# Four more 128-column dummy matmuls on TensorE ahead of the first projection

## The chip, the cores and the metric

The kernel runs on one core of one Trainium2 chip. The metric is device time in microseconds (us). The profile's granted clock does not show the start: in the view by windows it reads 1.00 from the first us on, while the first 4 us of matmuls come at half the later rate, so "slow" and "full" clock below are read from the spacing of matmuls.

Names of engines in the profile: PE is TensorE (matmuls), PEld its weight loads, DVE VectorE, ACT ScalarE, POOL GpSimd, SP the queue that issues most DMAs. L939 is line 939 of the kernel.

## The reference, cut to what matters

```python
xn = layernorm(x)                                   # x: 2048 x 512, bf16
out = x + ssm(xn) + (gelu(xn @ w_gate) * (xn @ w_up)) @ w_down
# ssm: a diagonal complex scan over 2048 steps, with projections into and out of the state
```

Only the beginning matters here: the first 128-row tiles of `x` are centered, transposed, and multiplied by the gate and up weights, which are 512 x 1376 and arrive by DMA in slices of 128 rows ("k slices").

## The kernel before

TensorE has nothing to compute for the first 4 us. It is kept busy with matmuls of constants: seven warm-up matmuls of 512 columns, then `fill(n)`, which is n matmuls of 128 columns. One dummy stands ahead of the first transpose and four behind it.

```python
nwarm = 7
...
PE(fwarm, d_pe([512] * nwarm) * 1.6, [], [BANK[wb]], "warm")      # L932
def fill(n):
    def f(e):
        ins_ = None
        for _ in range(n):
            ins_ = e.matmul(PS[wb][:, 0:128], ones, ones, start=True, stop=True)   # L939
        return ins_
    PE(f, 56.0 * n, [], [BANK[wb]], "fill")
...
ch(V(... tensor_reduce(SUM0, X[0]) ...))       # DVE: sum of the first x tile, L965
ch(cent(0, 0), cent(0, 1))                     # DVE: centers it, L960
fill(1)
ch(cent_T(0, 0, 1, 7, "V"))                    # PE: transpose "T0", L679; DVE copies it out, L688
ch(cent(1, 0), cent(1, 1))
fill(4)
...
ks(0, 0, [0], True)                            # PE: first projection, k slice 0, L700
cent_T(1, 0, 1, 6)
ks(0, 0, [1])
cent_T(0, 1, 4, 7)
...
for j in range(2):
    ks(1, j, [0, 1])                           # k slice 1
...
cent_T(2, 0, 4, 7)                             # four transposes
for j in range(2):
    ks(2, j, [0, 1])                           # k slice 2: "the third slice"
```

These loads go out on the SP queue, in this order (x tile 1 goes out on ScalarE's); GT_k (L700) waits for the gate and the up weights of its slice:

```python
ld_x0(0)
...
for k in range(KD):                            # KD = 4
    if k in (1, 3):
        ld_x0((k + 3) // 2)                    # x tile 2 ahead of slice 1, x tile 3 ahead of slice 3
    ld_wk(WG, WGc, ins["B_w_gate"], k)         # 128 KB each
    ld_wk(WU, WUc, ins["B_w_up"], k)
```

PE and the SP queue keep program order. The order on the other engines is chosen by the kernel's own scheduler from declared durations (the 56.0 * n above).

## Time and profile before

| | before |
|---|---|
| time, median of 3 runs | 177.44 us (177.3 to 177.45) |
| span of the profiled execution | 175.7 us (its time: 176.98 us) |
| PE busy | 172.1 us, 98% of the span |

From the page of the kernel before: the span, PE's line of part 1 (busy us, share, instructions), and the engines of the chain that ended last in part 4.

```profile
span 175.7 us, 2494 instructions
...
PE 172.1 (98%) x868; PEld 84.0 (48%) x883; DVE 159.8 (91%) x279; ACT 95.5 (54%) x185; POOL 10.7 (6%) x24
...
PE 98%; issue 1%; DVE 0%
```

PE is the chain. A change at the start counts only as far as it moves everything behind it. The timeline of PE in the first 11 us (columns: start, duration in us, engine, line, operation, out<-in, shape, count):

```profile
0.77 3.15 PE L932 MATMUL PS<-const-bfloat16-1.0 128*128 128x512 bf16 x7 [0.77 <-PEq L1089]
3.71 0.31 PE L939 MATMUL PS<-const-bfloat16-1.0 128*128 128x128 bf16 x1
3.87 0.29 PE L679 MATMUL PS<-arena 128*128 128x128 bf16 x1
3.95 0.51 PE L939 MATMUL PS<-const-bfloat16-1.0 128*128 128x128 bf16 x4
4.57 0.38 PE L700 MATMUL PS<-arena 128*128 128x256 bf16 x2
...
6.95 0.39 PE L679 MATMUL PS<-arena 128*128 128x128 bf16 x4
7.42 2.75 PE L700 MATMUL PS<-arena 128*128 128x512 bf16 x12
...
11.10 0.38 PE L711 MATMUL PS<-arena 128*128 128x512 bf16 x1
```

Matmuls overlap: a duration is a latency (219 ns for each of the four transposes at 6.95), and the distance between starts is the rate (56 ns). The four transposes that begin at 6.95 have their last start at 7.12, so the next matmul could start at 7.18. It starts at 7.42. That is the wait for the third slice: by the trace's landing times its up weights land at 7.288 (a load has landed when the last update of its semaphore has come). The dummies by themselves (the view of one line; duration in ns, minimum, median and maximum):

```profile
L939 PE MATMUL PS<-const-bfloat16-1.0 x5: 218/284/314, 3.7 to 4.2; 128*128 128x128 bf16 x5
```

314 ns is a dummy at the slow clock and 218 ns one at the full clock, so in this execution the clock opened within the run of dummies. The single starts put it between 4.16 and 4.24. The slow spacing is 107 ns for 128 columns and the full one 56; the Trainium skill, "TensorE: Matmul & The Clock Gate", section "Back-to-back issue gap", gives N / 1.2 and N / 2.4 + 2.5 ns, which is 107 and 56, and this trace agrees. In the chain of waits the tail then runs without an interruption of more than 0.05 us (the longest pieces: start, us, what):

```profile
7.42 2.75 PE PS L700 x12
10.40 0.86 PE PS L700 x4
11.26 6.93 PE PS L711 x40
18.24 5.13 PE PS L842 x23
```

### The profile page before, as it was taken

The numbers are of one execution on the slowest core, as the hardware profiler recorded it, in microseconds if no ns is written. First come the engines' busy times: TensorE is split into PE (matmuls) and PEld (weight loads), VectorE is DVE, ScalarE is ACT, GpSimd is POOL, SyncE is SP. The second block draws the span as 40 slices with busy tenths as digits, with TensorE's granted clock in tenths as the row PEclk, the third lists the DMA queues.
The fourth block names the chain that finished last, engine by engine and source line by source line (L and its number), as shares of the span: only waits on it lengthen the run. The fifth ranks groups of instructions, "written<-read, shape, count | busy, mean of one in ns | idle before, by whom it ended". The sixth has DMA issues, their size and how long they took to land.

```text
span 175.7 us, 2494 instructions
## 1 busy us (share of the span) xinstructions
PE 172.1 (98%) x868; PEld 84.0 (48%) x883; DVE 159.8 (91%) x279; ACT 95.5 (54%) x185; POOL 10.7 (6%) x24
## 2 busy tenths in 40 slices
PE   8999999999999999999999999999999999999995
PEld 3545564644544444444644444444464444444454
DVE  6987999996999989889899999989999899999941
ACT  5476677899876898383576792000667970000000
POOL 3122030201000000002100000000000000000000
DMA  5899999695998000002015000002001000000311
GB/s 155 241 320 174 215 178 222 126 132 113 191 298 225 0 4 2 0 30 85 8 39 111 1 0 0 4 0 90 30 0 30 4 0 0 0 0 0 120 64 60
DMA packets 32420, 14.36 MB, mean 82 GB/s; under 512 B 23736, under 2 KB 32408, under 8 KB 32408
## 3 DMA queue, kind: packets, MB, share of 16 engines
q1 hardware_dynamic: 32240, 14.07, 35.5%
q8 instruction: 7, 0.11, 0.3%
q10 hardware_dynamic: 168, 0.13, 0.2%
q14 instruction: 5, 0.04, 0.1%
HBM read 6.46 MB, written 2.10 MB: 49 GB/s over the span
## 4 chain that ended last, share of the span: by engine, by line
PE 98%; issue 1%; DVE 0%
PE PS L883 37%; PE PS L842 32%; PE PS L748 16%; PE PS L711 4%; PE PS L700 3%; PE PS L816 3%; PE PS L932 2%; PE PS L679 1%; PE PS L939 0%; DVE arena L901 0%
## 5 line engine op out<-in xcount | busy, mean ns | idle before, releaser
L883 PE MATMUL PS<-arena 128*128 128x512 bf16 (+3 forms) x317 | 65.9, 366 | 0.3
L842 PE MATMUL PS<-arena 128*128 128x512 bf16 x257 | 57.1, 379 | 0.4
L883 PEld LDWEIGHTS PS<-arena 128*128 128x128 bf16 (+1 forms) x323 | 30.8, 98 | 35.2
L842 PEld LDWEIGHTS PS<-arena 128*128 128x128 bf16 x264 | 25.8, 98 | 30.2
L786 DVE TENSOR_TENSOR_SCAN arena<-arena 128x512 bf16<-128x512 f32 x32 | 38.9, 1255 | 0.0
L857 ACT ACTIVATE arena<-PS 128x512 bf16<-128x512 f32 x33 | 19.8, 599 | 25.8 <-DVE arena L901 16.7
L748 PE MATMUL PS<-arena 128*128 128x512 bf16 (+1 forms) x134 | 28.0, 366 | 0.1
L861 ACT ACTIVATE arena<-PS 128x512 bf16<-128x512 f32 x33 | 19.8, 600 | 5.1 <-PE PS L842 5.1
L875 ACT ACTIVATE PS<-arena 128x512 f32<-128x512 bf16 (+2 forms) x17 | 9.6, 581 | 19.7 <-DVE arena L901 19.0
L748 PEld LDWEIGHTS PS<-arena 128*128 128x128 bf16 x136 | 13.3, 98 | 14.1
L757 ACT ACTIVATE arena<-PS 128x512 bf16<-128x512 f32 x32 | 17.7, 592 | 2.1 <-PE PS L748 2.1
L901 DVE TENSOR_TENSOR arena<-PS,arena 128x512 bf16<-128x512 f32 (+2 forms) x17 | 10.9, 653 | 6.4 <-PE PS L883 6.4
L863 DVE TENSOR_TENSOR arena<-arena 128x512 bf16<-128x512 bf16 x33 | 13.1, 416 | 1.7 <-ACT arena L861 1.6
L775 DVE TENSOR_TENSOR arena<-arena 128x4096 bf16<-128x4096 bf16 (+1 forms) x5 | 9.2, 1859 | 0.8 <-ACT arena L606 0.8
L773 DVE TENSOR_TENSOR arena<-arena 128x4096 bf16<-128x4096 bf16 (+1 forms) x5 | 9.2, 1859 | 0.1
L798 DVE TENSOR_TENSOR arena<-arena 128x4096 bf16<-128x4096 bf16 x4 | 9.2, 2288 | 0.1
L799 DVE TENSOR_TENSOR arena<-arena 128x4096 bf16<-128x4096 bf16 x4 | 9.1, 2284 | 0.0
L720 ACT ACTIVATE arena<-PS,arena 128x256 bf16<-128x256 f32 (+1 forms) x16 | 6.6, 448 | 3.9 <-PE PS L700 2.1
L610 DVE BATCH_NORM_STATS2 arena<-arena 128x6 f32<-128x512 bf16 x12 | 7.7, 679 | 0.1
L711 PE MATMUL PS<-arena 128*128 128x512 bf16 (+1 forms) x40 | 7.1, 336 | 0.0
L723 DVE SCALAR_TENSOR_TENSOR arena<-PS,arena 128x256 bf16<-128x256 f32 (+1 forms) x16 | 6.3, 445 | 0.5 <-PE PS L700 0.5
L700 PE MATMUL PS<-arena 128*128 128x512 bf16 (+1 forms) x28 | 6.2, 349 | 0.2
(96 smaller groups left out, 124.6 us busy)
## 6 DMA issues: line engine op xcount, KB each, us to landing
out_dram<-arena SPq DMA_DIRECT2D x15, 128.0 KB, 1.7
arena<-in_A_x_dram SPq DMA_DIRECT2D x3, 512.0 KB, 5.3
arena<-in_B_w_down_dram SPq DMA_DIRECT2D x1, 1280.0 KB, 7.2
arena<-in_B_w_gate_dram SPq DMA_DIRECT2D x4, 128.0 KB, 3.0
arena<-in_B_w_up_dram SPq DMA_DIRECT2D x4, 128.0 KB, 3.1
arena<-in_B_w_gate_dram SPq DMA_DIRECT2D x1, 480.0 KB, 6.5
arena<-in_B_w_up_dram SPq DMA_DIRECT2D x1, 480.0 KB, 7.4
arena<-arena SPq DMA_TRANSPOSE x25, 3.1
```

The costliest lines, as they stand in the source:

```text
L700: PE(lambda e: e.matmul(dst, XCd(j, k), WGU[:, ws[0]:ws[-1] + 1, k, f0:f1], start=first, stop=k == KD - 1, skip_group_check=True), d_pe([w ...
L711: ins_ = e.matmul(dst, XCd(j, k), WGU[:, :, k, f0:f1], start=(k == 0), stop=(k == KD - 1))
L748: ins_ = e.matmul(PS[bank][:, 128 * j0:128 * j1], BBT[c][dk].ap[:, 128 * s:128 * (s + 1)], XNT[b].ap[:, dk, 128 * j0:128 * j1], start=(dk ...
L757: GATE["evBu"] = ACT(lambda e, bank=bank, k3=k3, s=s, c=c: e.activation(SSc[k3][s][c].ap, PS[bank][:, :], ACTF.Copy), d_act(512), [BANK[ba ...
L786: V(lambda e, g=g, rb=rb, init=init: e.tensor_tensor_scan(g.ap, rb, g.ap, init, ALU.mult, ALU.add), d_dve_scan(512), [g, PA[RRr]] + ([CARc ...
L842: ins_ = e.matmul(PS[bank][0:m, c0:c1], W.ap[:, dk, 128 * ft:128 * ft + m], XNT[b].ap[:, dk, c0:c1], start=(dk == 0), stop=(dk == KD - 1))
L857: GATE["last_gelu"] = ACT(lambda e, bg=bg, kk=kk, m=m: e.activation(GG[kk].ap[0:m, :], PS[bg][0:m, :], ACTF.Gelu_apprx_tanh), d_act(512), ...
L861: ACT(lambda e, bu=bu, kk=kk, m=m: e.activation(UPB[kk].ap[0:m, :], PS[bu][0:m, :], ACTF.Copy), d_act(512), [BANK[bu]], [UPB[kk]], "evU")
L863: V(lambda e, kk=kk, m=m, ft=ft, k2=k2: e.tensor_tensor(HTt[k2][ft].ap[0:m, :], GG[kk].ap[0:m, :], UPB[kk].ap[0:m, :], ALU.mult), d_dve_tt ...
L875: ACT(lambda e: e.activation(PS[bank][:, c0:c1], X[tt].ap[:, c0:c1], ACTF.Copy), d_act(c1 - c0), [X[tt]], [BANK[bank]], "seed")
L883: ins_ = e.matmul(PS[bank][:, c0:c1], l_[:, 128 * j:128 * (j + 1)], r_[:, c0:c1], start=False, stop=last and n == len(ops) - 1, skip_group ...
L901: V(lambda e: e.tensor_tensor(OUTB[ko].ap[:, c0:c1], PS[bank][:, c0:c1], XD[tt].ap[:, c0:c1], ALU.add), d_dve_1x(c1 - c0), [BANK[bank], XD ...
```

## The change

Two dummies are added in each of the two gaps. The intent, as I read it, is to leave PE less idle while it waits, in the hope of an earlier or safer full clock.

```diff
         ch(cent(0, 0), cent(0, 1))
-        fill(1)
+        fill(3)
         ch(cent_T(0, 0, 1, 7, "V"))
         ch(cent(1, 0), cent(1, 1))
-        fill(4)
+        fill(6)
```

## The prediction

> What bounds the kernel now. TensorE does: the page gives PE 172.1 us busy of a 175.7 us span (98%), and the chain of waits that ended last is PE for 98% of the span. From 11.10 us on the chain shows PE without any gap over 0.05 us. So a change at the start is worth what it moves that 11.10 us, and nothing else.
>
> What the start looks like (PE in the timeline of the first 11 us). Seven warm-up matmuls run from 0.77 us, 427 ns apart; the first dummy starts at 3.71; the transpose T0 at 3.87, released by the first centering on DVE; four dummies from 3.95 to 4.24 (starts 107, 106 and 74 ns apart); then PE idles until the first projection at 4.57, which waits for DVE's copy of the transpose (4.20 to 4.43). The 74 ns step and the fall of a dummy's duration from 314 to 218 ns put the change to the full clock at 4.17 to 4.24 us, 3.4 us after the first matmul. The Trainium skill, "TensorE: Matmul & The Clock Gate", Part 1, says that about 3.4 us of sustained activity opens the clock gate; this trace agrees. From 4.57 us on everything already runs at full speed (256 columns 108 ns apart). So the dummies have nothing left to win here, in this execution: before 4.17 they can't open the clock sooner, since the warm-up has been dense since 0.77.
>
> What is added. Two dummies ahead of T0, at the slow clock: 107 ns each. They'd run at 3.82 and 3.92, so T0 starts at about 4.03 in place of 3.87: 0.16 us late, as there was only 0.055 us of room. The DVE copy and the first projection slide with it, to about 4.73. Two dummies behind T0: 56 to 107 ns each; they end before 4.60, still ahead of 4.73, so they cost nothing by themselves. PE work, slot time: about 0.33 us in all; nothing is removed, no DMA moves. The order on the other engines should stay as it is.
>
> What of it is on the critical path. The 0.16 us slide runs through the first and second k slices, until PE must wait for the third slice of the up weights. Landing times in the trace: its DMA lands at 7.29 us; PE's last transpose was issued at 7.12 and would have let the next projection start at 7.18, but it starts at 7.42. So PE holds 0.25 us of slack there, more than the slide of 0.16 us, and DMA issues do not depend on PE this early. I expect the projection at 7.42 to stay, and the tail at 11.10 to stay within 0.05 us.
>
> Predicted: 177.45 us, with a range of 177.0 to 178.0 us; faster by over 2% 0.015, within 2% 0.97, slower by over 2% 0.015.
>
> What would show the steps right: in the profile after, nine dummies in place of five; T0 at 4.0 to 4.1; the first projection at 4.65 to 4.8; the clock change still near 4.2; the projection ahead of which PE idled still at 7.4; the forty-matmul group at 11.1; a span of 175.5 to 176.2.
>
> What would make it wrong: the clock change falling later in the timed runs than in this profiled one (176.98 us against 177.44 in the timed ones hints at variation), where denser dummies could open it earlier and win some tenths, up to half of a 3.4 us window; a third-slice landing that is earlier in the timed runs, so that the 0.16 us shows; or the scheduler putting DVE and ScalarE work in another order, which could move either way by some tenths.

## The result, and the profile after

| | before | after |
|---|---|---|
| time, median | 177.41 us (177.3 to 177.45, 6 runs) | 177.36 us (177.15 to 177.66, 6 runs) |
| ratio | | 1.0000, 95% interval 0.9987 to 1.0013 |
| span of the profiled execution | 175.7 us | 176.3 us (its time: 177.62 us) |

A ratio is the mean time of one kernel's runs over that of the other's in the same rounds, so it is not quite the ratio of the medians. Here the means are 177.39 and 177.39 us: the same, with an uncertainty of about 0.23 us (0.13% of 177). The page after:

```profile
span 176.3 us, 2502 instructions
...
PE 172.8 (98%) x872; PEld 84.9 (48%) x887; DVE 159.7 (91%) x279; ACT 95.5 (54%) x185; POOL 10.7 (6%) x24
...
PE 98%; issue 1%; DVE 0%
```

The span is 0.6 us longer, although the times are equal. So the two profiled executions differ by more than the two kernels do, and the first question is by what. PE's timeline after:

```profile
0.77 3.15 PE L932 MATMUL PS<-const-bfloat16-1.0 128*128 128x512 bf16 x7 [0.77 <-PEq L1089]
3.71 0.53 PE L939 MATMUL PS<-const-bfloat16-1.0 128*128 128x128 bf16 x3
4.03 0.31 PE L679 MATMUL PS<-arena 128*128 128x128 bf16 x1
4.14 0.85 PE L939 MATMUL PS<-const-bfloat16-1.0 128*128 128x128 bf16 x6
4.78 0.63 PE L700 MATMUL PS<-arena 128*128 128x256 bf16 x2
...
7.80 0.39 PE L679 MATMUL PS<-arena 128*128 128x128 bf16 x4
8.02 2.75 PE L700 MATMUL PS<-arena 128*128 128x512 bf16 x12
```

The first projection's two matmuls take 0.63 us here and 0.38 before: they run at the slow clock. All nine dummies do too:

```profile
L939 PE MATMUL PS<-const-bfloat16-1.0 x9: 314/314/314, 3.7 to 4.7; 128*128 128x128 bf16 x9
```

The single starts put the opening of the clock between 6.06 and 6.26, 2 us later than before. The third slice starts at 8.02, without a wait: the last transpose of the four starts at 7.97, one spacing of 56 ns earlier. The tail moves by what the third slice moves, and nothing changes behind it (a piece of this view starts where the one before it ends, hence 8.19 here for the start at 8.02):

```profile
8.19 2.59 PE PS L700 x12
11.00 0.86 PE PS L700 x4
11.86 6.93 PE PS L711 x40
18.84 5.13 PE PS L842 x23
```

The up weights of the third slice landed at 7.752 in this execution and at 7.288 before. Had PE been on time, the third slice would have started 0.135 us behind the landing, as it did before (7.423 - 7.288), at 7.887. So of the 0.60 us between the two profiles, 0.46 is a later DMA landing, and 0.13 is PE arriving later than that landing. Neither is obviously the dummies' work. Twelve experiments were made to settle it.

### The profile page after: what moved, and what is told of

Its sections match the earlier page's. It is cut to its first block, busy times and chain, and to the rows that moved or that the text cites. A ratio compares the mean times of both kernels' runs of the same rounds, so it can differ in the third digit from the quotient of the medians.

```text
span 176.3 us, 2502 instructions
## 1 busy us (share of the span) xinstructions
PE 172.8 (98%) x872; PEld 84.9 (48%) x887; DVE 159.7 (91%) x279; ACT 95.5 (54%) x185; POOL 10.7 (6%) x24
## 4 chain that ended last, share of the span: by engine, by line
PE 98%; issue 1%; DVE 0%
PE PS L883 37%; PE PS L842 32%; PE PS L748 16%; PE PS L711 4%; PE PS L700 3%; PE PS L816 3%; PE PS L932 2%; PE PS L679 1%; PE PS L939 1%; DVE arena L901 0%
## 5 line engine op out<-in xcount | busy, mean ns | idle before, releaser
L748 PE MATMUL PS<-arena 128*128 128x512 bf16 (+1 forms) x134 | 28.0, 366 | 0.1
L711 PE MATMUL PS<-arena 128*128 128x512 bf16 (+1 forms) x40 | 7.1, 337 | 0.0
L723 DVE SCALAR_TENSOR_TENSOR arena<-PS,arena 128x256 bf16<-128x256 f32 (+1 forms) x16 | 6.3, 445 | 0.7 <-PE PS L700 0.7
L700 PE MATMUL PS<-arena 128*128 128x512 bf16 (+1 forms) x28 | 6.8, 373 | 0.0
```

What stands on the lines that cost most here:

```text
L700: PE(lambda e: e.matmul(dst, XCd(j, k), WGU[:, ws[0]:ws[-1] + 1, k, f0:f1], start=first, stop=k == KD - 1, skip_group_check=True), d_pe([w ...
L711: ins_ = e.matmul(dst, XCd(j, k), WGU[:, :, k, f0:f1], start=(k == 0), stop=(k == KD - 1))
L748: ins_ = e.matmul(PS[bank][:, 128 * j0:128 * j1], BBT[c][dk].ap[:, 128 * s:128 * (s + 1)], XNT[b].ap[:, dk, 128 * j0:128 * j1], start=(dk ...
```

## The experiments

Three theories at the outset. **A** (the prediction's): the dummies push the first transpose T0 back, and the wait for the third slice takes that up. **B**: the dummies themselves move the moment at which the clock opens. **C**: that moment varies from one execution to the next, whatever the dummies. From the first four runs theory A was put in numbers, as **A2**, which the later expectations quote.

The first four ran on one chip, the next four on another, the last four on a third; each group shares 11 runs of the kernel before (medians 177.45, 177.34 and 177.19 us).

### The kernel before again, and the changed kernel again

No edit in either.

> The kernel before, unchanged, as a control. Theory A (my prediction: dummies don't move the clock; T0's slide of 0.16 us is taken up by the wait for the third weight slice): time ratio 1.000, the clock in the profile opens at 4.2 us as in the first profile of this kernel, PE idles again about 0.2 us ahead of 7.4. Theory C (the moment when the clock opens varies from one execution to the next, whatever the dummies): the clock opens at another moment than 4.2 us in this profile, anywhere between 4.2 and about 7.6, and the span follows it, up to 0.6 us longer.

Measured: 177.47 us median (177.2 to 178.41), ratio 1.0011 (0.9986 to 1.0037) against itself: this is the resolution of five rounds. In this profile the clock opened between 4.28 and 4.34 us, so it does not tell A from C. But the span is 176.2 us, not 175.7. The third slice started at 7.839, exactly 0.135 us behind a landing at 7.704; PE's wait ahead of it had grown from 0.25 to 0.55 us (last transpose at 7.235). So the weights' landing alone moved the unchanged kernel by 0.42 us at this point; 0.16 more came behind it, 0.14 of it as a wait of PE that ended at 32.9 us.

> The changed kernel again. Its first profile opened the clock at 6.1 to 6.2 us, 2 us later than before's 4.2. Theory B (the dummies themselves move the opening): it opens at 6.1 to 6.2 again and the single times stay about 177.4. Theory C (it varies by execution): it opens at some other moment; single times spread over 0.5 us (177.15 to 177.66 as in the first six runs), ratio to before within 0.2%.

Measured: 177.28 us median (177.05 to 177.71), ratio 0.9996 (0.9977 to 1.0015). The clock opened between 3.92 and 4.12, not at 6.1 to 6.2. Theory B, as expected here, fails: with the same nine dummies the clock opened 2 us sooner. The first x tile landed late (3.065 us against 2.816), and T0 at 4.12 was waiting for it and not for the dummies: the timeline shows the three dummies of the first gap done starting by 3.92.

### Each half of the change, and no dummies at all

```diff
-        fill(1)            # first gap only
+        fill(3)
```

> Only the first half of the change: two more dummies ahead of T0. Theory A: T0 at 4.03 in place of 3.87, first projection at 4.7, ratio 1.000 (within 0.1%), tail group at 11.1 if the clock opens by 4.3. If nothing took the slide up, +0.16 us (+0.09%).

Measured: 177.35 us median, ratio 1.0001 (0.998 to 1.0023). T0 at 4.037 and the first projection at 4.756, as expected. The clock opened between 4.25 and 4.35. The last transpose started at 7.313, so PE would have been ready at 7.37; the weights landed at 7.406 and the third slice started at 7.541, again landing + 0.135. A wait of 0.17 us was left. This execution shows the absorption that the prediction described: T0 late, third slice set by the landing. But the dummies made T0 late by only 0.04 us in it (4.037 against 2.940, the landing of the first x tile, plus 1.056, which the DVE work behind it takes). The tail was at 11.21, not at 11.1, because the landing was later.

```diff
-        fill(4)            # second gap only
+        fill(6)
```

> Only the second half of the change: two more dummies behind T0. With the clock open by about 4.3 they end before the first projection can start (DVE's copy sets it): cost 0. With a late clock (it opened at 5.3 to 6.2 us in six of ten profiles) six dummies of 107 ns end 0.03 us or so too late. Ratio 1.000, within 0.1%.

Measured: 177.33 us median, ratio 1.0006 (0.9984 to 1.0029). The clock opened between 5.95 and 6.05. The first projection started 0.72 us behind T0; without any dummies and with a late clock, the next run, it is 0.70. The price of the second half is at most some hundredths. The profiled execution was a long one (178.36 us), in part because its third slice came at 7.97, and in part (0.84 us) for a reason far from the change, which its view of waits for line 748 names:

```profile
  DMA arena<-arena: 0.7, 1
```

A transpose by DMA of the second block of x landed at 33.55 us, and PE stood still until 33.69. It is a second wait for a DMA, 25 us behind the third slice, which appears in some executions (0.14 us in the control above) and not in others.

```diff
-        fill(1)
...
-        fill(4)
```

> No dummies at all in the two gaps: PE then idles from about 3.71+0.43 to the first projection. Theory A and C: T0 still at 3.87, first projection at 4.57, ratio 1.000 within 0.1% on the mean, as PE has slack later anyway. Theory B (denser PE opens the clock sooner): the clock opens up to 3.4 us later on average, ratio 1.002 to 1.006.

Measured: 177.51 us median (177.22 to 178.9), ratio 1.0017 (0.9989 to 1.0045). The clock opened between 5.94 and 6.14. T0 at 4.005 waited for the first x tile, which landed at 2.950. One profile with a late clock does not show that the dummies' absence made it late, as the kernel with nine dummies was as late; the ratio is inside the control's interval. Left undecided by itself.

### Twenty more: how much does a dummy cost?

The declared length of the fill stays that of one dummy, so that the order of everything else stays.

```diff
-        fill(1)
+        fill(21, 1)        # 21 issued, declared as 1
```

> 21 dummies ahead of T0 in place of 1, the same declared length, so the order of everything else stays. Theory A2 (from the first runs: the third weight slice starts at the later of PE's arrival, T0 + 3.30 us, and the landing of its last DMA + 0.135 us; T0 starts at the later of the end of the dummies and the landing of the first x tile + 1.056 us): the dummies end at about 5.14 if the clock opens at 4.2, T0 at 5.14, PE arrives at about 8.4, later than landing + 0.135 (7.34 to 7.89 so far), so the third slice starts without a wait and the time rises by 0.5 to 1.1 us, ratio 1.003 to 1.006. A theory in which dummies are free, as PE is never late: ratio 1.000. If each dummy cost its slot in full: 5 of 107 ns and 15 of 56 ns, 1.4 us, ratio 1.008.

Measured: 178.64 us median (177.95 to 178.86), ratio 1.0064 (1.0044 to 1.0085); by the means, 178.52 against 177.36, 1.16 us longer. PE's timeline:

```profile
3.71 2.20 PE L939 MATMUL PS<-const-bfloat16-1.0 128*128 128x128 bf16 x21
5.75 0.22 PE L679 MATMUL PS<-arena 128*128 128x128 bf16 x1
...
8.77 0.39 PE L679 MATMUL PS<-arena 128*128 128x128 bf16 x4
8.99 2.75 PE L700 MATMUL PS<-arena 128*128 128x512 bf16 x12
```

The mechanism is as expected and the size a little above it. The third slice started at 8.99 without a wait, 1.49 us later than landing + 0.135 (7.368 + 0.135), and behind it nothing differs from before. The size exceeds the expected range because the clock opened late again, between 5.42 and 5.52, so most of the twenty added dummies took 107 ns. T0 is 1.80 us later than where the landing of the x tile (2.898, plus 1.056 of DVE work and hand-over) would have let it start; the time rose by 1.16. So dummies are neither free nor paid in full: the room ahead of the third slice takes a part.

This run says something else as well. PE issued matmuls back to back from 0.77 us on, and the clock still took 4.65 us to open. Denser work did not make it early.

### Taking the wait away

The third and fourth slices multiply by the second slice's weights (a wrong result), and the waits for the later weights are dropped. The order of all engines is the same.

```diff
-  WGU[:, ws[0]:ws[-1] + 1, k, f0:f1], start=first
+  WGU[:, ws[0]:ws[-1] + 1, min(k, 1), f0:f1], start=first
...
+        late = [S.last_w[c[k].name] for c in (WGc, WUc) for k in (2, 3)]
+        for op in S.ops:
+            if op.tag == "GK":
+                op.deps = [d for d in op.deps if d not in late]
```

> The kernel before, in which the third and fourth slices of the first projection multiply by the second slice's weights, so that nothing waits for the later weights; wrong results on purpose. Theory A2: the gap of 0.25 us ahead of the third slice is gone, PE goes through from T0 to T0 + 3.2 to 3.4 us, the tail group begins 0.1 to 0.5 us sooner, ratio 0.997 to 0.9995. If the landing is not what ends that gap: the gap stays, ratio 1.000.

Measured: 177.59 us median, ratio 1.0009 (0.9994 to 1.0024). The expectation of a gain failed; the measured interval leaves at most 0.1 us of it. In its profile the gap is gone, but there was nothing to win: the clock opened between 6.03 and 6.19, PE reached the third slice at 7.775, and the weights, landed at 7.29, would have let it start at 7.425. Two further things stood ready to take a gain back: a new wait of 0.08 us ahead of the tail group, seen in this run and the next and in no other, and the later DMA waits described above.

> The same for the changed kernel; wrong results on purpose. Theory A2: with the wait gone the dummies' slide is no longer taken up: the third slice starts at T0 + 3.2 to 3.4 us with T0 at 4.03 or later, so 0 to 0.16 us later than in the kernel before without the wait, as far as the first x tile lands early; on time the two differ by less than can be told (0.1%). Ratio to before 0.997 to 1.000.

Measured: 177.41 us median (5 runs), ratio 1.0008 (0.9993 to 1.0024). The clock opened between 5.32 and 5.44; the third slice started at 7.672, when landing + 0.135 would have been 7.54. T0 to third slice is 3.64 us, outside the expected 3.2 to 3.4, because part of it ran at the slow clock. In this execution PE then waited 0.34 us near 18.5 us for the last transpose of the first x block (landed 18.55; the view of waits names DVE's L723, whose semaphore was only looked at behind that one). The pair does not measure the dummies' slide. What it shows is that "PE has slack ahead of the third slice" is at most a property of executions with an early clock, and not of the kernel.

### Making the wait certain

First, one load moved ahead of the third slice's weights:

```diff
-            if k in (1, 3):
-                ld_x0((k + 3) // 2)
+            if k in (1, 2):
+                ld_x0(k + 1)
```

> The kernel before with the fourth x tile loaded ahead of the third weight slice and not behind it; the order of all engines is the same. Theory A2: the third slice's last weights land one transfer of 128 KB later, about 0.35 us; the third slice starts at that landing + 0.135 us, and the time rises by 0.2 to 0.4 us (ratio 1.001 to 1.0025), more in executions with an early clock. If PE's own work sets the time: 1.000.

Measured: 177.46 us median, ratio 1.0009 (0.9991 to 1.0027): inconclusive. The landing came at 7.545, which is within what the ordinary order shows (7.18 to 7.75). The third slice started at 7.680, landing + 0.135.

Then two loads moved, in the queue's order alone, in both kernels:

```diff
         S.schedule()
+        q = S.order["sync"]
+        first = [S.last_w[X[3].name], S.last_w[WGc[3].name]]
+        for op in first:
+            q.remove(op)
+        at = q.index(S.last_w[WGc[2].name])
+        q[at:at] = first
         S.emit()
```

> The kernel before with the fourth x tile and the fourth slice's gate weights loaded ahead of the third slice's, so that the third slice's last weights land two transfers (about 0.7 us) later, at 8.0 to 8.5; all engines but the DMA queue are unchanged. Theory A2: the third slice starts at that landing + 0.135 us whatever the clock does (arrival at most 8.0); time up by 0.3 to 0.8 us, ratio 1.002 to 1.0045, and the moment of the clock's opening no longer shows in it.

Measured: 178.07 us median, ratio 1.0042 (1.0023 to 1.0062), as expected. Its PE timeline, where the profile now names the wait:

```profile
4.67 0.38 PE L700 MATMUL PS<-arena 128*128 128x256 bf16 x2 [0.18 <-DVE arena L688]
...
7.11 0.39 PE L679 MATMUL PS<-arena 128*128 128x128 bf16 x4
8.43 2.75 PE L700 MATMUL PS<-arena 128*128 128x512 bf16 x12 [0.93 <-DMA arena<-in_B_w_up_dram]
```

> The same late landing with all four added dummies. Theory A2: the dummies only shorten the wait ahead of the third slice; it again starts at landing + 0.135 us, and the time is that of the run before this one within 0.1%. If the dummies cost their slide at the end, 0.05 to 0.16 us more.

Measured: 177.85 us median, ratio 1.0033 (1.0015 to 1.005). By the means it is 0.16 us below the run before it (177.91 and 178.08), inside the noise. Its timeline:

```profile
4.85 0.64 PE L700 MATMUL PS<-arena 128*128 128x256 bf16 x2
...
7.86 0.39 PE L679 MATMUL PS<-arena 128*128 128x128 bf16 x4
8.34 2.75 PE L700 MATMUL PS<-arena 128*128 128x512 bf16 x12
```

This is the clearest pair. The first execution had an early clock and five dummies, the second a late one (6.13 to 6.27; 0.64 us for the first two projections against 0.38) and nine. PE came to the third slice at 7.34 in the one and 8.08 in the other. Both waited for the landing, at 8.294 and 8.200, and started 0.135 us behind it. PE came 0.74 us later in the second, and nothing of it reached the third slice. Little of the 0.74 is the dummies' work: T0 waited for the first x tile in both (landed 2.970 and 3.079), so that the first gap cost nothing, and the late clock makes up most of the rest. The pair shows that the wait takes up a late PE, whatever made it late; it does not measure the dummies' slide.

The early clock of the first execution can be read from its dummies:

```profile
L939 PE MATMUL PS<-const-bfloat16-1.0 x5: 219/222/231, 3.7 to 4.3; 128*128 128x128 bf16 x5
```

The first of them, at 3.71, took 231 ns, where 311 to 314 is the slow clock. Its start is one slow spacing (427 ns for 512 columns) behind the last warm-up matmul. So the clock opened behind 3.71 and before T0 at 4.03.

### What the warm-up itself is worth

```diff
-            for _ in range(nwarm):
+            for _ in range(1):
...
-        fill(1)
...
-        fill(4)
```

> One warm-up matmul in place of seven and no dummies, the same order elsewhere. If PE work ahead of the first projection is what opens the clock, the opening moves to 7.2 us or later (T0 at about 3.9 plus 3.4 or more), and the third slice comes 0.5 to 2 us later; ratio 1.003 to 1.012. If the opening did not depend on PE's activity, 1.000.

Measured: 178.51 us median (177.83 to 179.01), ratio 1.0064 (1.0043 to 1.0085). PE idles 2.65 us ahead of T0, and the slow clock lasts through most of the first two slices (0.58 us for the first two projections, 2.12 for the six from 6.68):

```profile
4.01 0.29 PE L679 MATMUL PS<-arena 128*128 128x128 bf16 x1 [2.65 <-DVE arena L960]
4.70 0.58 PE L700 MATMUL PS<-arena 128*128 128x256 bf16 x2 [0.41 <-DVE arena L688]
...
6.68 2.12 PE L700 MATMUL PS<-arena 128*128 128x256 bf16 x6
8.64 0.39 PE L679 MATMUL PS<-arena 128*128 128x128 bf16 x4
```

The clock opened between 8.39 and 8.64. So dummy work does buy the clock, and removing warm-up and dummies costs 0.6%. Most of that should be the 3 us of warm-up: removing the dummies alone (1.0017, 0.9989 to 1.0045) showed no cost beyond its noise. No run removed the warm-up alone.

### All profiles side by side

Read from the traces' instruction and landing records. "x lands" is the first x tile; "opens" is the start of the last matmul that came one slow spacing (107 ns for 128 columns) behind the one before it, and the start of the next; "W lands" is the up weights of the third slice; "late" is how far behind W lands + 0.135 the third slice starts; "rest" is the span less the third slice's start. Times are in us. r1 to r12 are the experiments by number.

```
run     dummies  x lands  T0     opens         W lands  third slice  late   rest
before  1+4      2.816    3.873  4.16 - 4.24   7.288    7.423        0      168.24
r1      1+4      2.925    3.980  4.28 - 4.34   7.704    7.839        0      168.41
after   3+6      2.925    4.032  6.06 - 6.26   7.752    8.021        0.13   168.25
r2      3+6      3.065    4.123  3.92 - 4.12   7.208    7.498        0.16   168.24
r3      3+4      2.940    4.037  4.25 - 4.35   7.406    7.541        0      168.49
r9      1+6      3.001    4.059  5.95 - 6.05   7.178    7.973        0.66   169.08
r4      0+0      2.950    4.005  5.94 - 6.14   7.405    7.898        0.36   168.24
r5      21+4     2.898    5.755  5.42 - 5.52   7.368    8.993        1.49   168.24
r6      1+4      2.830    3.885  6.03 - 6.19   no wait  7.775        -      168.32
r7      3+6      2.882    4.037  5.32 - 5.44   no wait  7.672        -      168.65
r8      1+4      2.830    3.887  5.29 - 5.48   7.545    7.680        0      168.24
r11     1+4      2.970    4.026  3.71 - 4.03   8.294    8.429        0      168.24
r12     3+6      3.079    4.135  6.13 - 6.27   8.200    8.335        0      168.24
r10     none*    2.950    4.009  8.39 - 8.64   7.321    8.865        1.41   168.25
* and one warm-up matmul in place of seven
```

Three rules hold in all rows. T0 starts at the later of the end of the first dummies (4.03 for three of them) and the landing of the first x tile + 1.06. The third slice starts at the later of PE's own arrival and the landing + 0.135. Behind it the rest takes 168.24 us, plus what later waits add in some executions (0.07 to 0.84).

The column "opens" carries theory C. With the seven warm-up matmuls it runs from 3.71 to 6.27 in thirteen profiles. With nine dummies it is 3.92, 5.32, 6.06 and 6.13; with five, 3.71, 4.16, 4.28, 5.29 and 6.03; with seven, 4.25 and 5.95; with none, 5.94; with 25, 5.42 (the last slow start in each). There is no order by the number of dummies. The chip may have a part in it, which no run tests: on the chip of r5 to r8 all four opened late, at 5.29 to 6.03. But two of these, r6 and r8, have the same PE work up to there and still differ by 0.7 us. The Trainium skill, "TensorE: Matmul & The Clock Gate", Part 1, has an explanation that fits in part: activity is watched over a free-running window of 3413 ns, which does not begin with the kernel. That the window is what makes it vary is the page's account; the runs here show only the variation, 2.9 to 5.5 us behind the first matmul. In r2 and r11 the clock opened at most 3.35 and 3.25 us behind it, sooner than one whole window of activity.

## Why the prediction was right

**The total.** 177.45 us predicted, 177.36 measured, both well within 2%. The number was right, and a part of the reasoning was right for fewer executions than it claimed. The number tests little of it: had all 0.33 us of added work reached the end, 177.44 + 0.33 would have lain inside the stated range too.

**"T0 starts at about 4.03 in place of 3.87", and the first projection at 4.65 to 4.8.** Right: 4.03 and 4.78. But the size of the slide, 0.16 us, was read from one execution in which the first x tile landed earlier than in any later one (2.816 us). Over the fourteen profiles it landed between 2.816 and 3.079, and the slide that three dummies cause, 4.032 less the landing less 1.056 where that is positive, averages 0.06 us and is zero in three of them. The dummies mostly filled time in which PE was waiting for x anyway.

**"Two dummies behind T0 ... cost nothing by themselves."** Right to within 0.05 us: from T0 to the first projection it is 0.69 us in the profile before, 0.70 without any dummies, and at most 0.75 with six of them, all at the slow clock (the profile after).

**"The clock change still near 4.2."** Wrong for the profile after, 6.06 to 6.26. The failing step is "this trace agrees": one trace in which the clock opened 3.4 us behind the first matmul was taken for how the kernel behaves. The runs put the opening anywhere from 2.9 to 5.5 us behind it. So the reason given, that a warm-up dense since 0.77 us cannot have the clock before 4.17, fails as well: r2 and r11 had it by 4.12 and 4.03 with the same warm-up. Whether dummies move the average moment stays open. The last slow starts average 5.36 with nine dummies (four profiles) and 4.69 with five (five profiles), and each group spreads over more than 2 us.

**"PE holds 0.25 us of slack there ... the projection at 7.42 to stay, and the tail at 11.10 to stay within 0.05 us."** The mechanism was right, and shown: a third slice at landing + 0.135 as long as PE comes before it, in the first-gap run and the pair with the late landing. The dummies' own slide is seen taken up only in the first-gap run, where it was 0.04 us. As a number for every execution it was wrong. The landing itself moves (7.18 to 7.75 us with the ordinary order of loads), and PE is later than it with a late clock, or, as in the repeat of the changed kernel, when the first x tile and the first up weights land late (3.065 and 5.138 us, against 2.816 and 4.631). Among the seven profiles with ordinary loads, full warm-up and at most nine dummies, PE waited in three and came late in four. In the profile after the third slice was at 8.02 and the tail at 11.70, and the span of 176.3 us lay just outside the predicted 175.5 to 176.2.

**Why the time is the same, then.** Where the clock opens early, the slide of 0 to 0.16 us goes into the wait for the third slice's weights (the repeat of the changed kernel excepted, which had an early clock and late loads). Where it opens late, nothing takes it up, but the slide is on average 0.06 us, plus up to 0.05 from the second gap. Those sizes, an estimate from the table, are 0.03 to 0.06% of the time and below the 0.13% that the comparison of the two kernels resolves. The repeat (0.9996) agrees. The change gives nothing back either, because the clock does not open sooner for it as far as the profiles show.

**What stays open.** How often the clock opens late in the timed runs, of which there are no traces; why the landings vary; and why the first six runs of the kernel before spread over only 0.15 us, when 39 later ones spread over 1.48 us (176.93 to 178.41).

## What to carry to other kernels

Filler work in a gap that ends at a DMA landing costs nothing as long as it ends before the landing, and what it runs over once it doesn't (with 21 dummies, 1.49 of T0's 1.80 us reached the third slice); read both ends of the gap from several executions before trusting a slack of a tenth. A warm-up is worth having (0.6% here, together with the dummies), but filling its last gaps more densely showed no gain that these runs can resolve. When two profiles of near-identical kernels differ by more than their times do, profile the unchanged kernel again before explaining the difference.

## What the Trainium skill lacked or had wrong

- "TensorE: Matmul & The Clock Gate", Part 1, gives the transition's run-to-run variation as ±500 ns. With the same seven warm-up matmuls it fell between 3.71 and 6.27 us here, 2.9 to 5.5 us behind the first matmul: a range of about 2.5 us. (A note further on in that part, that one kernel showed 6, 11 or 14 slow matmuls, fits this better.)
- The same page, "Why this matters for your kernels", advises at least 4 us of continuous matmuls to reach the full clock. In the run with 21 dummies PE was dense from 0.77 us on and the clock opened only at 5.42 to 5.52, 4.65 us later at least, so 4 us would not have been enough.
- The same page, "Single matmul latency", gives (219 + N) / 1.2 ns at the slow clock, 289 ns for 128 columns. That holds for one that had waited (T0 at the slow clock took 286 to 289 in eight profiles); in a stream the dummies show 311 to 314, for which the section has no term. Its figure for the full clock, (398 + N) / 2.4, is 219 ns, and the traces show 218 to 219.
- I found no page that gives the time from a DMA's landing to the first matmul that waited for it: 0.135 us in all six profiles that waited for the third slice. It is no constant: in r2 the first projection with the up weights started 0.046 us behind their landing (5.138). There the weight load itself carried the wait; ahead of the third slice a separate semaphore instruction of 0.05 us did.
